# First chunk of a fused attention and MLP kernel: segments on 128 folded columns in PSUM banks of their own, four blocks by token half, grouped warm-up products, one listed order

## The chip, the cores and the metric

One NeuronCore of one Trainium2 chip runs the whole program. The metric is the device time of one execution in microseconds (us), as a median of several runs; smaller is better. The kernel before takes 912.23 us (three runs, 912.14 to 913.46).

## The reference

Sliding-window attention with a distance bias, then a two-layer MLP with squared relu, in float32 (the MLP's weights arrive as float64):

```python
B, H, S, D = 8, 8, 576, 64; window = 128
scores = q @ k.T / sqrt(D)
rel = pos[:, None] - pos[None, :]
scores = where((rel >= 0) & (rel < window), scores - slopes[h] * abs(rel), -1e9)
attn = softmax(scores)                       # per batch and head
x = (attn @ v).transpose(0, 2, 1, 3).reshape(B * S, H * D)   # 4608 x 512
out = (maximum(x @ w_in, 0) ** 2) @ w_out    # w_in 512 x 2048, w_out 2048 x 512
```

## The kernel before

The 4608 tokens form nine chunks of 512. Attention of a chunk is four head pairs; a pair has two segments of 256 queries. In the program's names, segment k = 0 to 7 belongs to the first chunk (pair k // 2, half k % 2 of the tokens), segments 8 to 15 to the second; q = 4 to 7 are the pairs of the second chunk and q = 8 is the first pair of the third. TensorE works in split precision: each product of float32 operands is three products of a high and a low part.

The MLP's first product of a chunk is sixteen blocks `g1` (one for each 128 columns of `w_in`; twelve products of 128 x 512), each followed by relu, square, a high part (`hh`) and a low part (`hl`). The second is sixteen blocks `g2`, twelve products each, summed in four PSUM banks. Sixteen weight units of 1 MB, `w` 0 to 15, arrive as float64 words on SyncE's queue and are turned into high and low parts in five steps `c` 0 to 4: a scaling on ScalarE (L204), a shift and a combine on VectorE (L206, L208), the high part on ScalarE (L210), the low part on VectorE (L212). A unit serves two blocks of `g1` or two of `g2`.

`start` records the first stage: attention of the first chunk, the MLP of the first chunk (`g1` 0 to 15, `g2` 0 to 13), the weights' conversion, attention of the second chunk and the scores of pair 8. `middle` records all that follows. Its first block of TensorE work is the last six products on the first chunk that the first stage leaves, then the second chunk's first `g1`; from there on the two kernels have the same work on TensorE. Every engine runs its instructions in the order in which they were recorded.

A first-chunk segment goes through `Wide`: scores `s` (L788) on up to 256 key columns per query block; four steps `u` (L798) that add a distance table to the scores in PSUM and take the row minimum; four exponentials `e` (L805) on ScalarE with their row sums; the reciprocals `r` (L436, L437); the scaling `n` (L818 on GpSimd, L816 on VectorE for one segment); transposes `z` (L825, L828) on TensorE; the copies `o` (L457, mostly ScalarE) and `m` (L832, VectorE) to SBUF; the product with the values `x` (L471); the high part `h` (L481, ScalarE) and the low part `l` (L484, VectorE). The segments run in the order 0, 1, 2 to 7. Pairs 4 to 8 use folded columns: the keys of a query's window lie in 128 columns by their position modulo 128; a copy `base` moves the scores to SBUF (L637, L644, ScalarE), and `fold` (L656, L660, VectorE) puts the older keys over the masked places. After the exponentials the folded tile goes through DRAM (`square`, `write`, `read`), and two selects (L508, GpSimd) part it into keys of the own and of the previous block, called `same` and `before`. `S` is a pair's scores (L584), `V` its product with the values (L520).

The order is set by a planner (`Plan.run`): each step has an engine, a duration, predecessors, a due time and the buffers it takes and frees, and a table of corrections `NUDGE`. One PSUM bank `g` serves `g1`; it is free when the relu has read it (L242). Warm-up products on zeros (`heat`, L160) fill TensorE in the first 32 us.

## Time and profile before

| what | value |
|---|---|
| time, median of 3 runs | 912.23 us (912.14 to 913.46) |
| profiled execution: span | 911.2 us, 1.0 us under that median |
| TensorE busy | 901.9 us of the span |
| VectorE, ScalarE, GpSimd busy | 579.5, 467.2, 259.6 us |
| granted TensorE clock | 1.00 throughout |

The page gives busy time for each engine, the span in 40 slices, and the chain that ended last. What matters here is where TensorE waits: it waits before 46 us and hardly after, so the stages have to be read apart. Other views give busy time in chosen stretches, single instructions in order of time, and the idle time ahead of groups of instructions with what ended it. An instruction's "us" includes a part that overlaps the next one's start; the distance between two starts is its pitch.

### The profile page before, as it was taken

Reading aid. Unit: us, or ns where it says so; the run is one execution under the profiler, and the core shown is the slowest. Engines: PE = TensorE matmul, PEld = TensorE weight load, DVE = VectorE, ACT = ScalarE, POOL = GpSimd, SP = SyncE. Lnnn points to the kernel's source line nnn. Section 1 sums busy time; section 2 is a strip of 40 time slices with the busy share of each in tenths; the row PEclk is TensorE's granted clock in tenths of the full one; section 3 lists DMA queues with packets and bytes.
Section 4 is the critical chain, followed back from the end, with each engine's and each line's share of the span. In section 5 each row is a group of like instructions: output and inputs, shape, how many; then the busy total and the mean of one; then the engine's idle time right before and its main releaser. Section 6 shows DMA issues by size and latency. Waiting matters only on the chain.

```text
span 911.2 us, 23218 instructions
## 1 busy us (share of the span) xinstructions
PE 901.9 (99%) x8500; PEld 799.2 (88%) x8500; DVE 579.5 (64%) x1596; ACT 467.2 (51%) x1321; POOL 259.6 (28%) x339
## 2 busy tenths in 40 slices
PE   9899999999999999999999999999999999999998
PEld 5688888888889999999999999999999999989997
DVE  6998882667776666565756665667666565654333
ACT  7898663566654445444544444445444454432222
POOL 4213235665522322213222322231322222230000
PEclk9999999999999999999999999999999999999999
DMA  9985226768888877877777778777887786667541
GB/s 347 404 312 171 88 62 210 243 211 275 296 278 293 292 253 260 262 246 221 233 279 247 216 236 267 250 227 243 271 258 229 244 261 195 193 207 224 171 126 47
DMA packets 137568, 212.95 MB, mean 234 GB/s; under 512 B 15216, under 2 KB 49392, under 8 KB 137456
## 3 DMA queue, kind: packets, MB, share of 16 engines
q1 hardware_dynamic: 137024, 210.96, 70.8%
q8 instruction: 68, 1.11, 0.5%
q10 hardware_dynamic: 432, 0.52, 0.2%
q14 instruction: 44, 0.36, 0.1%
HBM read 170.52 MB, written 40.89 MB: 232 GB/s over the span
## 4 chain that ended last, share of the span: by engine, by line
PE 95%; DVE 2%; DMA 1%; ACT 1%; issue 0%; POOL 0%; POOLq 0%; SPq 0%; DVEq 0%
PE acc L388 44%; PE chain L331 17%; PE rest L331 13%; PE g L233 9%; PE s L743 5%; PE g L756 2%; PE s L756 1%; PE at L520 1%; PE g L160 1%; DMA flow<-ws 1%; DMA pp<-way 0%; PE acc L471 0%; PE s L788 0%; PE acc L788 0%; DVE w L212 0%
## 5 line engine op out<-in xcount | busy, mean ns | idle before, releaser
L388 PE MATMUL acc<-hh,w 128*128 128x512 f32 x1152 | 405.3, 397 | 0.3 <-issue 0.3
L388 PEld LDWEIGHTS acc<-hh,w 128*128 128x128 f32 x1152 | 225.4, 196 | 39.5 <-issue 5.3
L388 PE MATMUL acc<-hl,w 128*128 128x512 f32 x576 | 227.4, 395 | 0.0
L336 DVE TENSOR_TENSOR four<-four,rest 128x256 f32<-128x256 f32 x112 | 47.2, 421 | 215.7 <-PE rest L331 214.6
L331 PEld LDWEIGHTS rest<-xu,flow 128*128 128x128 f32 x1008 | 143.8, 191 | 13.1
L508 POOL TENSOR_SCALAR_AFFINE_SELECT pp<-pp 128x512 f32<-128x512 f32 x128 | 95.5, 753 | 199.7 <-DMA pp<-way 163.3
L351 ACT COPY four<-chain 128x256 f32<-128x256 f32 x56 | 20.9, 373 | 251.4 <-PE chain L331 251.4
L331 PE MATMUL chain<-tees,flow 128*128 128x256 f32 x1008 | 147.5, 282 | 0.0
L331 PE MATMUL rest<-xu,flow 128*128 128x256 f32 x1008 | 146.7, 281 | 0.0
L441 POOL TENSOR_TENSOR t<-t,nm 128x512 f32<-128x512 f32 x64 | 69.6, 1090 | 256.8 <-DVE nm L437 162.5
L331 PEld LDWEIGHTS chain<-tees,flow 128*128 128x128 f32 x1008 | 132.2, 192 | 0.0
L388 PEld LDWEIGHTS acc<-hl,w 128*128 128x128 f32 x576 | 112.8, 196 | 12.8
L429 ACT ACTIVATE t<-t,nm 128x128 f32<-128x128 f32 x256 | 100.3, 395 | 8.9 <-DVE nm L422 8.3
L233 PE MATMUL g<-xu,w 128*128 128x512 f32 x384 | 95.2, 397 | 1.2 <-ACT r L242 1.2
L233 PEld LDWEIGHTS g<-xu,w 128*128 128x128 f32 x384 | 76.3, 209 | 14.3 <-ACT r L242 1.8
L422 DVE CUSTOM_DVE_ANT_0 t<-t,cst 128x128 f32<-128x128 f32 x256 | 63.1, 302 | 1.7
L251 DVE TENSOR_TENSOR hl<-r,hh 128x512 fp32r<-128x512 f32 x32 | 28.3, 883 | 43.1 <-ACT hh L249 43.0
L743 PE MATMUL s<-pp,v 64*64 64x128 f32 (+1 forms) x1792 | 52.3, 248 | 0.3 <-POOL pp L508 0.2
L331 PEld LDWEIGHTS chain<-xu,flow 128*128 128x128 f32 x336 | 48.7, 196 | 4.1
L656 DVE COPY_PREDICATED t<-cst,s 64x256 f32<-64x256 int32 x100 | 44.5, 445 | 11.8 <-PE s L743 5.4
L331 PE MATMUL chain<-xu,flow 128*128 128x256 f32 x336 | 49.4, 283 | 0.0
L429 ACT ACTIVATION_READ_ACCUMULATOR t<-t,nm 128x1 f32 x256 | 48.4, 189 | 0.0
(106 smaller groups left out, 1132.2 us busy)
## 6 DMA issues: line engine op xcount, KB each, us to landing
flow<-ws SPq DMA_DIRECT2D x392, 256.0 KB, 4.5
raw<-in_dram SPq DMA_DIRECT2D x32, 512.0 KB, 8.7
way<-pp SPq DMA_DIRECT2D x256, 64.0 KB, 2.2
pp<-way SPq DMA_DIRECT2D x64, 256.0 KB, 2.7
qk<-in_dram SPq DMA_DIRECT2D x32, 320.0 KB, 5.3
v<-in_dram SPq DMA_DIRECT2D x32, 320.0 KB, 4.6
qk<-in_dram SPq DMA_DIRECT2D x38, 256.0 KB, 5.1
out_dram<-o SPq DMA_DIRECT2D x35, 256.0 KB, 2.6
```

Source lines behind the costliest of these rows:

```text
L233: nc.tensor.matmul(g, w, xs[cc][:, part], start=i == 0, stop=i == 11)
L251: nc.vector.tensor_tensor(hl, r, hh.bitcast(F32), op=ALU.subtract)
L331: self.nc.tensor.matmul(to, w, x, start=start and k == 0, stop=k == 5, skip_group_check=True)
L336: add = lambda to, x: nc.vector.tensor_tensor(to, to, x, op=ALU.add)
L388: self.nc.tensor.matmul(self.acc[m], w, h, start=(f == 0 and i == 0), stop=(f == NF - 1 and i == 2))
L422: self.nc.vector.tensor_tensor_reduce(self.t[:, m], self.t[:, m], self.K.nrel(2 * self.p + m // 2), -0.125, BIG, ALU.add, ALU.min, self.nm ...
L429: return self.nc.scalar.activation(self.t[:, m], self.t[:, m], AF.Exp, bias=nm[:, 4 + m : 5 + m], scale=-1.0, accum_out=nm[:, m : m + 1],)
L441: self.nc.gpsimd.tensor_tensor(*(x.rearrange("p (j i) c -> p j i c", j=2) for x in (self.t, self.t)), self.rec.unsqueeze(3).to_broadcast([ ...
L508: nc.gpsimd.affine_select(to, self.own, pattern=[[-32 * sign, 4], [0, 4], [-sign, 32]], compare_op=op, fill=0.0, base=0, channel_multiplie ...
L656: nc.vector.copy_predicated(d, mask.unsqueeze(1).to_broadcast([64, 2, 2, 64]), e)
L743: yield self.nc.tensor.matmul(to, w, x, start=first and n < 2, stop=not first, skip_group_check=True)
L756: made = self.nc.tensor.matmul(to, w, x, start=not extra, stop=True, skip_group_check=True)
```

## The change

`Wide` becomes `Near`: the first chunk's segments use folded columns too. Scores are written by 64-row pieces, `fold` merges in PSUM, and `u` and `e` see 128 columns where they saw up to 256. The transposed tile is copied once (`o`), and two selects on GpSimd, `before` and `same`, make the two parts; the copy `m` is gone. Scores, transposes and value products have PSUM banks of their own (`low2`, `odd`, `sum1`) until the sums of `g2` take these banks over. The segments run as 0, 2, 4, 6 (first token half), then 1, 3, 5, 7. The tables `wide` (four loads of 256 KB) go; a select on GpSimd (`first`) makes a masked table from the shared one. For pairs 4 to 8 `base` goes too, and `merge` folds in PSUM.

```diff
+SEGMENTS = (0, 2, 4, 6, 1, 3, 5, 7)
+PSUBS = (0, 2, 12, 15)
+SUBS = (6, 7, 8, 9, 15, 16, 17, 21)
+HIGHS = (11, 15)
+HEATS = (7, 4, 4, 3, 8, 1, 3)
-HEAT = 16
-        (nc.gpsimd.tensor_copy if f in CASTS else nc.scalar.copy)(wh, flo)
-        nc.vector.tensor_tensor(wl, flo, wh.bitcast(F32), op=ALU.subtract)
+        (nc.gpsimd.tensor_copy if f in CASTS else nc.vector.tensor_copy if f in TRUNCS else nc.scalar.copy)(wh, flo)
+        (nc.gpsimd if f in PSUBS else nc.vector).tensor_tensor(wl, flo, wh.bitcast(F32), op=ALU.subtract)
...
+    def half1(self, u, s):
+        nc, cols = self.nc, slice(256 * s, 256 * s + 256)
+        g = self.g1.tile([128, 512], F32, name="g").rearrange("p (n t) -> p n t", n=2)
+        for n in range(2):
+            i = 0
+            for cc in range(NCC):
+                wl, wh = self.block(0, 2 * u + n, cc)
+                x = self.x[0, cc][:, :, cols]
+                for w, part in ((wh, 0), (wh, 1), (wl, 0)):
+                    nc.tensor.matmul(g[:, n], w, x[:, part], start=n == 0 and i == 0, stop=i == 11, skip_group_check=True)
...
+    def fold(self):
...
+        for h in range(2):
+            r = slice(64 * h, 64 * h + 64)
+            d = b[r, :, i, 64 * h : 64 * h + 64]
+            self.nc.vector.copy_predicated(d, self.K.mask[r].unsqueeze(1).unsqueeze(1).to_broadcast(list(d.shape)), e[r, :, i])
...
+    def unfold(self, own):
+        m = slice(1, 4, 2) if self.skip and not own else slice(0, 4)
+        to, sign = (self.own, -1) if own else (self.prev[:, m], 1)
+        self.nc.gpsimd.affine_select(
+            to, self.own[:, m], pattern=[[0, 2 if self.skip and not own else 4], [-sign, 128]], compare_op=ALU.is_ge if own else ALU.is_gt,
+            fill=0.0, base=0, channel_multiplier=sign,
+        )
...
+            P.add(n("before"), "Pool", 0.75 if sg else 0.4, (n("o"),), d - 1, do(G.unfold, False))
+            P.add(n("same"), "Pool", 0.75, (n("before"),), d - 1, do(G.unfold, True))
+            NF - 1: [("x", 6), ("x", 7)], ...
+            NF - 5: [("x", ends[1])], **{NF - 6 - u: [("g2", 2 * u + 1)] for u in range(HALVES)},
...
-            P.add(n("base"), "Activation", 0.6 if s else 1.3, (("S", q),) + first("base"), d + 5, do(C.begin, s), "t", "at" if s else None)
+            P.add(n("fold"), "DVE", 1.65 if late else 0.93, (("S", q),) + first("fold"), d, do(C.merge, s), "t")
...
-    return P.run()
+    return P.follow(ISSUE)
```

`half1` splits the first four blocks of `g1` by token half: `ga` 0 and 1 take two blocks each on tokens 0 to 255 (from segments 0, 2, 4, 6), `gb` 0 and 1 the same blocks on tokens 256 to 511; each is 24 products of 128 x 256. Their relu, square and parts are the steps `ha` and `hb`. In place of the planner's choice `start` follows a written list, `ISSUE`, so the order on every engine is fixed. The exponentials of pair 8 (eight `e`, sums and scaling) go from `start` to `middle`. The high part of two weight units moves to VectorE, three such steps come back from GpSimd to ScalarE, and the low parts of four units (`PSUBS`) and of several blocks (`SUBS`, `HIGHS`) go to GpSimd. Weight units 10 and 9 now lie where the parts of the first four blocks are kept, so their loads wait for `g2` 1 and 3. Thirty warm-up products in groups of 7, 4, 4, 3, 8, 1 and 3 stand where 32 stood in pairs.

On TensorE, where the first blocks begin, the kernel before has the scores of pair 4 (L584, cut here to their end), the last value product of the first chunk (L471, `pp`), `g1` 0 (`w_250`) and the first of pair 5's scores; `g1` 1 follows these:

```order
L584 MATMUL at<-qk 64x128
L584 MATMUL s<-qk 64x64
L471 MATMUL acc<-pp,v__242 64x128 x8
L233 MATMUL g<-xu,w_250 128x512 x12
L584 MATMUL at<-qk 64x128 x2
```

In the changed kernel the first half-token block `ga` 0 (L319, `w_224`) stands behind the value product of segment 1 (L567, `pw_98`), and the transposes of segments 5 and 7 (L932, `tw_95`, `tw_96`) and the value product of segment 3 (`pw_99`) stand behind it:

```order
L932 MATMUL odd<-cst,tw_94 128x128 x4
L567 MATMUL sum_117<-pw_98,v 64x128 x8
L319 MATMUL g<-xu,w_224 128x256 x24
L932 MATMUL at<-cst,tw_95 128x128 x4
L567 MATMUL sum_117<-pw_99,v 64x128 x8
L932 MATMUL odd<-cst,tw_96 128x128 x4
```

The first block has moved ahead of three value products and of pair 4's scores; the last of these products (segment 7) stands between `ga` 1 and `gb` 0, which is followed by pair 5's scores and `gb` 1.

On ScalarE the same stretch of the changed kernel, from the last exponential of segment 7 to its high part, reads as follows, in two pieces (L525 is `e`, L261 a weight's high part, L255 a weight's scaling, L553 is `o`, L577 is `h`, L299, L304 and L306 are relu, square and high part of `ha`; the names' numbers tell the units apart):

```order
L525 ACTIVATE tw_96,nm<-tw_96,nm 128x128
L261 CAST w_287<-raw_286 128x1024
L255 ACTIVATE raw_446<-raw_446 128x1024
L553 COPY pw_100<-at 128x512
L255 ACTIVATE raw_490<-raw_490 128x1024
L577 CAST xu<-sum_117 128x256
L553 COPY pw_101<-odd 128x512
L299 ACTIVATE r<-g 128x512
L304 ACTIVATE r<-r 128x512
L255 ACTIVATE raw_412<-raw_412 128x1024
L577 CAST xu<-sum_117 128x256
L306 CAST h_102<-r 128x2x256
```

and goes on with:

```order
L261 CAST w_342<-raw_341 128x1024
L255 ACTIVATE raw_370<-raw_370 128x1024
L299 ACTIVATE r<-g 128x512
L577 CAST xu<-sum_117 128x256
L304 ACTIVATE r<-r 128x512
```

The second fence goes on where the first ends; its L577 row is the high part of segment 7. In the kernel before, this high part stood behind the scalings of four units and one high part of a weight (L204 and L210) only:

```order
L204 ACTIVATE raw_355<-raw_355 128x1024
L481 CAST xu<-acc 128x256
L204 ACTIVATE raw_388<-raw_388 128x1024
L210 CAST w_292<-raw_291 128x1024
L481 CAST xu<-acc 128x256
L637 COPY t<-at 128x512
```

So seven scalings, three high parts of weights and four steps of `ha` now stand ahead of segment 7's high part, where four and one stood.

On SyncE's queue the first loads of the changed kernel are the first-half queries and keys, the table, the values, then weight unit 0 (`raw_223`), the second halves and unit 1 (`raw_286`):

```order
L167 DMA v__205<-in_dram 128x512
L249 DMA raw_223<-in_dram 128x1024 x2
L167 DMA qk<-in_dram 128x512 x3
L167 DMA qk__186<-in_dram 128x512
L249 DMA raw_286<-in_dram 128x1024 x2
```

Before, all loads of the first chunk and the four `wide` tables stood ahead of unit 0.

More of the change, by code (lines that the diff above doesn't have):

```diff
@@ L765, in two @@
             self.K.tc.add_manual_dep(made.ins, self.gate.ins.name, SYNC, reason="halves of the keys change banks")
-class Wide(Segment):
+class Near(Segment):
     def __init__(self, K, k):
         super().__init__(K, k)
-        self.skip = int(self.sg == 0)
-        self.first = [128 if self.skip and i == 0 else 0 for i in range(2)]
+        self.skip, self.turns = int(self.sg == 0), SEGMENTS.index(k)
     def scores(self):
@@ L824, in turn @@
         for m in range(4):
[L825 to L832 removed]
+            self.nc.tensor.transpose(self.z[:, m], self.t[:, m], self.K.ident)
@@ L857, in room, with follow @@
         self.count[name] = [0.0] * n
+    def follow(self, text):
+        names = [x[0] if len(x) == 1 else (x[0], *map(int, x[1:])) for x in (y.split(".") for y in text.split())]
+        assert sorted(names, key=str) == sorted(self.steps, key=str), set(names) ^ set(self.steps)
+        done = set()
+        for name in names:
+            engine, us, after, due, do, take, free, lag = self.steps[name]
+            assert done.issuperset(after), name
+            if do:
+                do()
+            done.add(name)
     def run(self):
@@ L874, in run @@
                     other = self.steps[a][0] != engine
-                    t = max(t, end[a] + HAND.get(self.steps[a][0], 0.15) * other + lag)
+                    t = max(t, end[a] + (HAND.get(self.steps[a][0], 0.15) if other else self.same * (engine in VECTOR)) + lag)
                 if any(not self.count[r] for r in take):
@@ L962, in start @@
-        P.add(n("h"), "Activation", 0.4, (n("x"),), d + 2, G.high)
-        P.add(n("l"), "DVE", 0.36, (n("h"),), d + 2, G.low, None, "xa")
+        after = [("q", c, p, 0), ("q", c, p, 1)][: sg + 1] + ([("s", SEGMENTS[i - 1])] if i else [])
+        chain = lambda s: ((s, SEGMENTS[i - 1]),) if i else ()
+        d, slot, turned = 4.0 * i, "sa" if i % 2 else "sc", "zp" if i % 2 else "at"
+        P.add(n("s"), "PE", 0.85 if sg else 0.92, tuple(after), d, G.scores, slot)
+        if not sg:
+            P.add(("first", p), "Pool", 0.5, ("nrel" if p else "near",), -1, do(K.table, p))
@@ new lines, in start @@
+        P.add(n("z"), "PE", 0.62, (n("n"),) + chain("z"), d - 3, G.turn, (turned, "pw"), "tw")
+        P.add(n("o"), *(("DVE", 0.6) if k in COPIES else ("Activation", 0.48)), (n("z"),), d - 2, G.out, None, turned)
+        P.add(n("before"), "Pool", 0.75 if sg else 0.4, (n("o"),), d - 1, do(G.unfold, False))
+        P.add(n("same"), "Pool", 0.75, (n("before"),), d - 1, do(G.unfold, True))
+        P.add(n("x"), "PE", 1.05 if sg else 0.82, (n("same"), ("v", c, p)) + chain("x"), d + 4, G.values, "xa", "pw")
@@ L964, in start @@
+        P.add(n("h"), "Activation", 0.27, (n("x"),), d + 2, G.high)
+        P.add(n("l"), "DVE", 0.34, (n("h"),), d + 2, G.low, None, "xa")
         if sg == 1:
@@ new lines, in start @@
+    for u in range(HALVES):
+        g = K.half1(u, 0)
+        P.add(("ga", u), "PE", 2.88, (*have(0), ("c", UNIT(0, 2 * u), n)) + ((("ga", u - 1),) if u else ()), GO, lambda g=g: next(g, None), "g")
+        after(("ha", u), 16 + u, g)
+    last, todo, f2 = {1: (), 2: ()}, [], 0
+    for u in range(HALVES):
+        todo.append(("gb", u))
+        if u:
+            todo += [("g2", f2), ("g2", f2 + 1)]
+            f2 += 2
+    for f in range(2 * HALVES, NF):
+        todo.append(("g1", f))
+        if f >= 2:
+            todo.append(("g2", f2))
+            f2 += 1
@@ L1280, in _consts @@
         cst[:, 256 + 128 * a : 384 + 128 * a] = -rel * (8 * slope(a))
-    later = r[:, None] < r[None, :]
-    near = [cst[:, 256 + 128 * a : 384 + 128 * a] for a in range(H)]
-    return np.concatenate([cst] + [np.where(late, t, np.float32(NEG)) for t in near for late in (later, ~later)], axis=1)
+    return cst
 def _arrays(q, k, v, moe_w_in, moe_w_out):
```

396 lines of the change are left out of this document (253 added, 143 removed), and 6 rows, old and new, of the table NUDGE.

## The prediction

> **What bounds the kernel now.** I looked first at busy time by stretch, because a mean over the span hides where TensorE waits. Columns are the stretch in us, its length, the busy time of PE, PEld, DVE, ACT and POOL, the granted clock, the DMA share and GB/s:
>
> ```profile
> 0.00:46.00 46.00, 41.14 (x392) 27.32 (x392) 36.67 (x136) 36.98 (x107) 14.93 (x19) 1.00 0.99 376
> 46.00:139.25 93.25, 93.17 (x627) 78.17 (x628) 80.07 (x171) 72.31 (x158) 29.73 (x35) 1.00 0.47 153
> 139.25:240.00 100.75, 100.75 (x878) 86.02 (x876) 59.64 (x147) 57.76 (x141) 59.79 (x70) 1.00 0.76 249
> ```
>
> From 46 us TensorE works without a pause: 93.17 of 93.25 us, then all of it. Time can only be won ahead of 46 us, and whatever is won there can be lost again by a wait behind it. The chain that ended last shows what follows that point (start, us, engine, line, count):
>
> ```profile
> 46.08 3.08 PE g L233 x12
> ...
> 106.60 2.80 PE acc L388 x12
> ...
> 110.87 3.15 PE g L233 x12
> ...
> 132.94 1.90 PE at L520 x32
> 134.84 4.41 PE acc L388 x18
> 139.25 2.79 PE g L233 x12
> ```
>
> At 46.08 the third `g1` begins. A block costs 2.80. A pair's scores cost 1.47 (from 106.60 + 2.80 to 110.87), a pair's value product 1.90. At 139.25 the second chunk begins; both kernels have the same TensorE work behind it. So I compare the moment at which **four `g1` blocks, all of the first chunk's attention and the scores of pairs 4 and 5** are done: before, these are done, by count of work, at 46.08 + 2 x 2.80 = 51.7 us. What is left from there is the same in both.
>
> TensorE's own order ahead of that point (the last value product, `g1` 0 and `g1` 1):
>
> ```profile
> 35.05 1.09 PE L471 MATMUL acc<-pp,v__242 128*64 128x128 f32 x16 [0.56 <-DVE xu L484]
> 36.08 3.21 PE L233 MATMUL g<-xu,w 128*128 128x512 f32 x12
> ...
> 42.25 3.09 PE L233 MATMUL g<-xu,w 128*128 128x512 f32 x12 [0.42 <-ACT r L242]
> ```
>
> The first block waits for the whole attention of the chunk. A value product takes 1.03.
>
> **The change: the new order to the same point.** ScalarE is the engine with the longest list up to there, so I add its pitches (start to next start) from its rows in order of time:
>
> ```profile
> 6.42 0.40 ACT L805 ACTIVATE tw<-tw,nm 128x128 f32<-128x128 f32 x1 [3.10 <-DVE nm L798]
> ...
> 13.15 0.59 ACT L457 COPY pp<-at 128x512 f32<-128x512 f32 x1 [0.17 <-PE at L825]
> 13.63 0.51 ACT L805 ACTIVATE tw<-tw,nm 128x256 f32<-128x256 f32 x1
> ...
> 16.71 0.37 ACT L481 CAST xu<-acc 128x256 fp32r<-128x256 f32 x1 [0.17 <-PE acc L471]
> 16.98 0.41 ACT L805 ACTIVATE tw<-tw,nm 128x128 f32<-128x128 f32 x1
> ...
> 22.82 1.15 ACT L204 ACTIVATE raw<-raw 128x1024 f32<-128x1024 f32 x1
> 23.86 0.57 ACT L457 COPY pp<-at 128x512 f32<-128x512 f32 x1
> ...
> 43.81 0.39 ACT L429 ACTIVATE t<-t,nm 128x128 f32<-128x128 f32 x1
> ...
> 44.20 0.39 ACT L429 ACTIVATE t<-t,nm 128x128 f32<-128x128 f32 x1
> ...
> 45.43 0.60 ACT L242 ACTIVATE r<-g 128x512 f32<-128x512 f32 x1
> 46.06 0.63 ACT L247 ACTIVATE r<-r 128x512 f32<-128x512 f32 x1
> 46.73 0.62 ACT L249 CAST hh<-r 128x512 fp32r<-128x512 f32 x1
> 47.25 1.16 ACT L210 CAST w<-raw 128x1024 fp32r<-128x1024 f32 x1
> ```
>
> `o` 0.48, `h` 0.27, a weight's scaling 1.04, an exponential on 128 columns 0.39, relu 0.63, square 0.67, high part 0.52; a weight's high part 1.16 less the same overlap of 0.11, 1.05. An exponential on 256 columns took 0.49 to 0.51 in its own row, so the 32 exponentials are also shorter than before.
>
> *The start.* Rows of TensorE and of VectorE's narrow fold:
>
> ```profile
> 1.30 3.88 PE L160 MATMUL g<-zero 128*128 128x512 bf16 x8 [1.30 <-DVE zero L155]
> 5.11 0.93 PE L788 MATMUL s<-qk 64*128 64x128 f32 x8
> ...
> 39.98 0.30 DVE L660 COPY_PREDICATED t<-cst,s 64x128 f32<-64x128 int32 x1
> ```
>
> Seven warm-up products instead of eight end at 1.30 + 7/8 x 3.88 = 4.7; scores 0.93; from their end to the first exponential it was 6.42 - 6.04 = 0.38; two folds add 0.65. First exponential: **6.7** (6.42 before).
>
> *To the first block `ga` 0.* It stands behind segment 1's value product, which needs segment 1's `o`. Ahead of and with that `o` ScalarE has 24 exponentials, five `o`, three `h`, two scalings and one high part: 9.4 + 2.4 + 0.8 + 2.1 + 1.05 = 15.7. To this come three waits. (a) Segment 2's reciprocals stand on VectorE ahead of segment 4's first `u`, and wait for segment 2's last exponential; so segment 4's first exponential is late by a reciprocal (0.35), a `u` (0.22) and handovers: 0.9. (b) Unit 0 has to land for its scaling. The loads:
>
> ```profile
> 0.00:10.00 10.00, 7.95 (x38) 3.16 (x38) 4.22 (x27) 5.07 (x17) 1.12 (x6) 1.00 0.83 282
> 10.00:20.00 10.00, 10.00 (x90) 6.85 (x90) 8.04 (x45) 9.32 (x36) 7.49 (x7) 1.00 1.05 398
> 20.00:30.00 10.00, 10.00 (x101) 7.19 (x100) 9.16 (x29) 9.25 (x29) 4.82 (x5) 1.00 1.03 404
> 30.00:40.00 10.00, 8.71 (x108) 6.59 (x106) 9.29 (x18) 7.68 (x13) 1.50 (x3) 1.00 1.03 405
> ...
> 40.26 1.32 ACT L204 ACTIVATE raw<-raw 128x1024 f32<-128x1024 f32 x1 [0.85 <-DMA raw<-in_dram]
> ```
>
> Up to unit 0 the new queue holds 3.80 MB (2.75 of queries, keys, values and tables, 1.05 of weights; 5.4 before). At 2.82 MB by 10 us and 398 GB/s these have moved by 12.5. Landing comes later: the unit that ScalarE waited for at 40.26 had 14.0 MB up to its end, and 14.9 had moved by 40, a lag of 2.1 us. Bounds 12.5 and 14.6; I take 13.4, nearer to the lower end, since the queue is short at that time. The scaling's turn comes at 12.2, so 1.2 (0.3 to 2.4); segments 2, 4 and 6's `o` and exponentials are queued behind it, and GpSimd's selects wait for these. (c) Unit 1 ends 2.1 MB later, at 18.6; its turn comes at 18.6 as well: 0 (to 1.2). With 0.3 for small handovers `o` ends at 6.7 + 15.7 + 0.9 + 1.2 + 0.3 = 24.8.
>
> GpSimd then does a select, a scaling (segment 3's) and a select before segment 1's value product:
>
> ```profile
> L818 POOL TENSOR_TENSOR tw<-tw,nm 128x512 f32<-128x512 f32 x4 | 4.2, 1043 | 0.0
> ...
> L441 POOL TENSOR_TENSOR t<-t,nm x64: 1042/1046/2022, 50.3 to 798.2; 128x512 f32<-128x512 f32 x64
> ...
> L508 POOL TENSOR_SCALAR_AFFINE_SELECT pp<-pp x128: 727/727/1581, 61.7 to 808.7; 128x512 f32<-128x512 f32 x128
> ```
>
> (the last two: minimum, median, maximum in ns). 0.73 + 1.04 + 0.73 and four handovers of 0.15: 3.1. Value product 1.03, so **`ga` 0 begins at 29.0**, 7 us ahead of `g1` 0 before.
>
> *From there TensorE's own work sets the time.* A half-token block has 24 products of 256 columns, priced by a group of six:
>
> ```profile
> 280.43 0.72 PE chain L331 x6
> ```
>
> 4 x 0.71 = 2.84. `ga` 0, two sets of transposes (0.5 each, an estimate: half of a value product's 16 records), three value products, pair 4's scores and `ga` 1: 2.84 + 1.0 + 3.1 + 1.47 + 2.84 = 11.2, so segment 7's value product ends at 40.2. Its `h`, `l` (0.34 by VectorE's pitch) and handovers, 1.1: 41.3. ScalarE's list up to that `h` is 32 exponentials, eight `o`, eight `h`, seven scalings, three high parts and four steps of `ha`: 12.5 + 3.8 + 2.2 + 7.3 + 3.15 + 2.45 = 31.4; with the waits above and 0.7 for segment 5's `o`, whose transposes now stand behind `ga` 0, it ends at 41.2, and `l` at 41.7. The two chains meet; I take 41.6 for `gb` 0. `gb` 0, pair 5's scores and `gb` 1 are 7.15, with 0.25 until a relu frees the one bank `g`: **49.0**, against 51.7.
>
> *Behind that point* TensorE has the same work, and 2.7 us less for everyone else. Two waits can take some of it. Units 9 and 10 now load only when `g2` 3 is done (49.0 + 5 x 2.80 = 63.0). Unit 9's scaling stands on ScalarE behind the square of `g1` 5, at about 67.5; behind it stand five other steps (2.7) and the relu that frees the bank for `g1` 7: 67.5 + 1.04 + 2.7 + 0.63 = 71.9, where `g1` 7's turn comes at 63.0 + 3 x 2.80 + 1.90 = 73.3, so there is 1.2 of room with a handover. Time to landing for these loads:
>
> ```profile
> DMA to landing us min/median/max: 3.8/8.7/11.8
> ```
>
> With little else on the queue then, I take 4.5 (bounds 3.8 and 8.7: nothing, or 3.0 on TensorE). And pair 7's value product stands 6 blocks, 1.90 and 1.47 behind its scores, 20.2, where it had 132.94 - 110.87 = 22.1; the chain between loses a copy to SBUF for each half (about an `o` each, 1.0 in all) and TensorE did not wait for it before, so I put it 0.3 late, with bounds of 0 and 0.9. I charge 0.6 for both: gain **2.1 us**.
>
> Costed at nothing: the warm-up products (TensorE waits there anyway; 0.49 each otherwise); `base` gone behind 46 us, where no wait of TensorE's hangs on it; VectorE's folds, covered by the removed copies `m` and by low parts that go to GpSimd; pair 8's exponentials in `middle` (ScalarE 57.8 of 100.75 us busy there; 3.1 without that cover).
>
> [...] GpSimd's operations above ran up to 2022 and 1581 ns, twice their minimum. [...]
>
> **The rivals.** Forecast, 912.23 - 2.1 = 910.1, chance 0.40 (909.0 to 911.2 by itself).
> *ScalarE hardly waits* (unit 0 lands by queue time, handovers hide): `ga` 0 some 2 us earlier and ScalarE 2.5 earlier, and nothing is given back: 907.3. For it: its rows before show waits of 0.17 only. Chance 0.23.
> *Weights land late*: units 0 and 1 at the upper ends cost 1.2 + 1.2 ahead of everything: 912.5. For it: the lag at 40.26. Against: the queue is shorter. Chance 0.15.
> *The gain is won and given back*: unit 9 or the way through DRAM makes TensorE wait 1.5: 911.6. Chance 0.10.
> *Slower: GpSimd becomes the bound*. Two selects a segment and the low parts go there; at the longest durations the three operations ahead of `ga` 0 cost 0.98 + 2 x 0.85 = 2.7 more and an earlier scaling 0.98, and `ga` 0 begins that much later: 913.8. It decides from 2.1 us in sum, about 0.5 for each of the four. Against: the scalings of the first 46 us took 1043. Chance 0.12.
>
> **How the numbers follow.** A measurement of this kernel can tell 0.2%, 1.8 us, from no change. Below 910.4 lie two thirds of the forecast's chance and the second case: 0.27 + 0.23 = 0.50. Within lie the rest of the forecast and two cases: 0.13 + 0.15 + 0.10 = 0.38. Slower by more: 0.12, though half of that case ends near its point of decision. The range 907.0 to 913.4 leaves out some 0.05 at the fast end and half of the slow case, and takes in the bounds of the landing.
>
> **What would show it.** First exponential near 6.7; unit 0's scaling waiting for its load about 1 us; `ga` 0 at 29, `gb` 0 at 41 to 42, `gb` 1's end at 49; TensorE without a pause from there to `middle`, whose first `g1` begins at about 137.1. It is wrong if `gb` 0 begins beyond 44 (GpSimd's or the weights' rows say which), or if TensorE pauses behind 49 for `r`, `raw` or `pp`.

## The result and the profile after

The changed kernel takes **918.37 us** (median of six runs, 915.38 to 920.52) against 912.92 for the kernel before beside it (six runs, 912.14 to 914.69): ratio 1.0057, 95% interval 1.0038 to 1.0076. It is slower by 0.57%, where 910.1 with a range up to 913.4 was predicted. The profiled execution took 917.32 us with a span of 915.6, so 4.4 us more than the profile before. Its six runs spread over 5 us, those of the kernel before beside them over 2.6.

First the same three stretches as before (stretch, length, busy time of PE, PEld, DVE, ACT, POOL, clock, DMA share, GB/s):

```profile
0.00:46.00 46.00, 40.66 (x463) 30.21 (x467) 34.35 (x150) 36.95 (x105) 25.00 (x33) 1.00 0.83 315
46.00:139.25 93.25, 91.58 (x677) 77.00 (x674) 70.19 (x167) 55.89 (x123) 35.66 (x32) 1.00 0.55 181
139.25:240.00 100.75, 98.27 (x858) 83.26 (x858) 61.28 (x141) 58.63 (x151) 62.80 (x73) 1.00 0.71 231
```

Behind 46 us TensorE no longer works through: it lacks 1.7 us of the second stretch and 2.5 of the third, where it lacked 0.1 and nothing. What it waited for, over the whole span (total, times, longest):

```profile
PE acc L466 <- ACT o L477: 2.5, 1, 2.5
PE g L284 <- ACT r L299: 1.7, 2, 1.3
PE s L897 <- DVE raw L257: 1.5, 1, 1.5
...
PE s L845 <- issue: 0.5, 1, 0.5
PE acc L466 <- issue: 0.5, 1, 0.5
```

L466 is a product of `g2`, L477 the copy of a finished PSUM bank to SBUF ahead of its store, L299 the relu. "Issue" means that the profile shows nothing that was waited for. The chain that ended last shows where this stands against the kernel before (start, us, engine, line, count):

```profile
29.52 3.79 PE g L319 x24
38.00 3.10 PE g L319 x24
42.13 3.79 PE g L319 x24
47.28 3.10 PE g L319 x24
50.38 2.80 PE acc L466 x12
...
139.71 2.79 PE g L284 x12
...
150.78 2.77 PE g L284 x12
153.58 0.61 ACT r L299
154.21 0.64 ACT r L304
154.87 0.62 ACT hh L306
155.48 0.49 ACT o L477
156.02 2.52 PE acc L466 x9
...
164.06 2.97 PE acc L466 x12
```

At the point that the prediction compares, the end of `gb` 1, the new kernel stands at 50.38 against 51.7: **1.3 us ahead**. At the second chunk's first `g1` it stands at 139.71 against 139.25: **0.5 behind**, so 1.8 went in between. The last row is the `g2` block behind the first visit of attention; in the kernel before it began at 160.64:

```profile
160.64 3.00 PE acc L388 x12
```

Now it is 3.4 behind. By 280 us it has won back 0.5 of that, and from there to 690 us the distance stays at 2.9; it grows by 0.6 and 0.9 at the two "issue" rows, which stand at 698 and 722 us, and is 4.3 at the end.

The loss at 153.58 reads thus: TensorE has finished a `g1` and its next product needs the PSUM bank of the first chunk's last output block. The copy that empties this bank stands on ScalarE behind relu, square and high part of that very `g1`. In the kernel before, the same copy (L399) stood one block earlier, at 150.64, ahead of the relu at 153.12:

```profile
150.64 0.59 ACT L399 COPY o<-acc 128x512 f32<-128x512 f32 x1 [1.13 <-DMA out_dram<-o]
153.12 0.60 ACT L242 ACTIVATE r<-g 128x512 f32<-128x512 f32 x1 [1.89 <-PE g L233]
```

The copy is the planner's work, in `middle`. The change gave `middle` pair 8's exponentials, sums and scalings, and so pair 8's write and read come later on SyncE's queue (143.80 instead of 139.77), with the stores of the output behind them (151.92 instead of 147.68). A copy needs one of four output buffers. By the planner's count two are held by early copies of weight blocks (GpSimd, to the same buffers) and two by the first two copies of the chunk, whose stores now come later; so none was free in time.

The loss at 102 us:

```profile
99.26 1.22 ACT L255 ACTIVATE raw<-raw 128x1024 f32<-128x1024 f32 x1 [2.37 <-DMA raw<-in_dram]
...
101.90 0.59 ACT L299 ACTIVATE r<-g 128x512 f32<-128x512 f32 x1
```

Weight unit 15's scaling waits 2.37 us for its load, and the relu that frees the bank `g` is queued behind it; TensorE loses 1.3. The load had been issued at 92.43, on SyncE's queue behind two writes and two reads of the way through DRAM. The remaining 0.4 of the L299 row is the same at 75 us, where unit 9's scaling waits 1.53 for its load.

### The profile page after: what moved, and what is told of

It reads as the page before. It is cut to its first block, busy times and chain, and to the rows that moved or that the text cites. A ratio compares the mean times of both kernels' runs of the same rounds, so it can differ in the third digit from the quotient of the medians.

```text
span 915.6 us, 23440 instructions
## 1 busy us (share of the span) xinstructions
PE 901.0 (98%) x8618; PEld 801.1 (87%) x8618; DVE 571.6 (62%) x1611; ACT 453.5 (50%) x1297; POOL 280.2 (31%) x355
## 3 DMA queue, kind: packets, MB, share of 16 engines
q8 instruction: 69, 1.13, 0.5%
## 4 chain that ended last, share of the span: by engine, by line
PE 92%; DMA 4%; ACT 1%; DVE 1%; SPq 1%; issue 1%; ACTq 0%; POOLq 0%; DVEq 0%
PE acc L466 43%; PE chain L406 18%; PE rest L406 13%; PE g L284 7%; PE s L845 5%; PE g L858 2%; DMA raw<-in_dram 2%; PE g L319 2%; PE s L858 1%; DMA way<-pp 1%; DMA qk<-in_dram 1%; DMA cst<-in_dram 1%; PE sum L567 1%; PE at L616 0%; PE at L680 0%
## 5 line engine op out<-in xcount | busy, mean ns | idle before, releaser
L466 PE MATMUL acc<-hh,w 128*128 128x512 f32 x1120 | 395.4, 398 | 3.0 <-ACT o L477 2.5
L466 PEld LDWEIGHTS acc<-hh,w 128*128 128x128 f32 x1120 | 219.3, 196 | 42.2 <-issue 6.1
L466 PE MATMUL acc<-hl,w 128*128 128x512 f32 x560 | 221.2, 395 | 0.0
L537 POOL TENSOR_TENSOR t<-t,nm 128x512 f32<-128x512 f32 x64 | 67.6, 1059 | 243.8 <-DVE nm L533 150.7
L466 PEld LDWEIGHTS acc<-hl,w 128*128 128x128 f32 x560 | 109.8, 196 | 12.0
L525 ACT ACTIVATE t<-t,nm 128x128 f32<-128x128 f32 x256 | 100.4, 395 | 9.6 <-DVE nm L500 9.0
L284 PE MATMUL g<-xu,w 128*128 128x512 f32 x336 | 83.0, 396 | 1.7 <-ACT r L299 1.7
L284 PEld LDWEIGHTS g<-xu,w 128*128 128x128 f32 x336 | 66.8, 209 | 13.0 <-ACT r L299 2.4
L500 DVE CUSTOM_DVE_ANT_0 t<-t,cst 128x128 f32<-128x128 f32 x216 | 52.8, 300 | 1.7
L845 PE MATMUL s<-pp,v 64*64 64x128 f32 (+1 forms) x1792 | 52.3, 248 | 0.7 <-issue 0.5
L589 DVE STREAM_TRANSPOSE pp<-t 128x512 f32<-128x512 f32 x64 | 45.2, 707 | 9.0 <-POOL t L537 5.8
L525 ACT ACTIVATION_READ_ACCUMULATOR t<-t,nm 128x1 f32 x256 | 48.6, 190 | 0.0
L299 ACT ACTIVATE r<-g 128x512 f32<-128x512 f32 x32 | 19.2, 599 | 53.3 <-PE g L284 44.9
```

The costliest lines, as they stand in the source:

```text
L284: nc.tensor.matmul(g, w, xs[cc][:, part], start=i == 0, stop=i == 11)
L466: self.nc.tensor.matmul(self.acc[m], w, h, start=(f == 0 and i == 0), stop=(f == NF - 1 and i == 2))
L500: self.nc.vector.tensor_tensor_reduce(self.t[:, m], self.b[m] if self.b else self.t[:, m], self.K.nrel(2 * self.p + m // 2), -0.125, BIG, ...
L525: return self.nc.scalar.activation(self.t[:, m], self.t[:, m], AF.Exp, bias=nm[:, 4 + m : 5 + m], scale=-1.0, accum_out=nm[:, m : m + 1],)
L537: self.nc.gpsimd.tensor_tensor(*(x.rearrange("p (j i) c -> p j i c", j=2) for x in (self.t, self.t)), self.rec.unsqueeze(3).to_broadcast([ ...
L589: nc.vector.transpose(squares.rearrange("p b m c -> p m b c"), self.t.rearrange("p m (b c) -> p m b c", c=32))
```

## Experiments: the two waits

Theory A: the late copy costs most of it. Theory B: unit 15's scaling costs 1 to 1.3. Rival C: the loss lies in the early part or in contention, and these waits are only where it shows. Beside all of the runs below but `copy_soon` the kernel before took 913.4.

**Pair 8 back in the first stage** (`e8_back`); `middle` is the kernel before's again:

```diff
-HAND = {"SP": 2.0, "PE": 0.3, "free": 0.0}
+HAND = {"SP": 2.0, "PE": 0.25, "free": 0.0}
...
-t.17.2 t.17.3 same.14 ... t.16.3 g1.15
+t.17.2 t.17.3 e.17.0 e.17.1 e.17.2 e.17.3 same.14 ... t.16.3 r.17 n.17 e.16.0 e.16.1 e.16.2 e.16.3 r.16 n.16 g1.15
...
-            first = min(ready, key=lambda r: (r[0], r[1], rank[r[2]]))
+            first = min(ready, key=lambda r: (r[0], r[1], str(r[2])))
...
-        chain(8, s, 0.0)
+        turned(8, s, 4.0 + 3 * s, ())
```

The edit also sets back a hand-over time of the planner (`HAND`) and its rule for ties. With these two alone set back, singly or together, the planner, which needs no chip, still puts the copy where the changed kernel has it; so it is pair 8's steps that move it.

> Pair 8's exponentials, sums and scalings stand in the first stage again, and the later stage plans as in the kernel before, so the copy-out of the first chunk's last bank stands on ScalarE right behind the other copy and not behind one more block's relu, square and high part. Theory A (this order costs the wait of 2.5 us and some 0.5 around it): the wait of TensorE for that copy is 0.2 or less, and the time is 918.4 - 3.0 = about 915.4. Theory B (unit 15's scaling ahead of a relu) alone: 918.4 unchanged. Rival C (the loss is in contention on GpSimd and VectorE or in the loads, wherever the copy stands): 918, the lost time shows in other waits.

Measured: 914.03 us, ratio 1.0011 (0.9996 to 1.0026), no wait for the copy.

**The same part alone, put into the kernel before** (`e8_alone`: the reverse edit, with the changed kernel's `middle`):

> The kernel before with one part of the change alone: pair 8's exponentials, sums and scalings in the later stage, planned as in the changed kernel. Theory A: TensorE waits about 2.5 us for the late copy here too, and the time is 912.9 + 3 = about 915.9. Theories B and C: 912.9, no change, since nothing else moves.

Measured: 917.44 us, ratio 1.0044 (1.0028 to 1.0061), with the wait:

```profile
PE acc L388 <- ACT o L399: 2.5, 1, 2.5
```

Done alone, this part makes the kernel before 4.0 us slower; undone, it makes the changed one 4.3 us faster. Handing pair 8's steps to `middle` is what costs, as theory A has it, and the early part isn't needed for it. Yet a wait of 2.5 us costs 4. Where the rest goes, three stretches of `e8_alone` show (the clock is the third number from the right):

```profile
151.97:155.38 3.41, 0.93 (x5) 0.47 (x4) 0.69 (x2) 2.33 (x4) 2.74 (x3) 1.00 0.98 368
155.38:158.80 3.42, 3.42 (x9) 2.68 (x10) 0.60 (x2) 0.00 (x0) 1.30 (x2) 0.50 0.77 291
158.80:162.21 3.41, 3.41 (x30) 2.62 (x32) 0.00 (x0) 0.24 (x1) 0.19 (x1) 1.00 0.47 174
```

TensorE was busy in 0.93 of 3.41 us; for the next 3.42 its granted clock is 0.50: another 1.7 us lost. The changes of the clock in a trace lie a whole number of stretches of 3.41 us apart (in `heat_less`, further on, it changes at 8.72, 15.54, 22.38 and 25.78 us). In the profiled execution of the changed kernel, counted back from the fall that its trace has just behind the end, at 916.45 us, the same wait lay across two such stretches, and the clock stayed at 1.00:

```profile
151.86:155.28 3.42, 1.68 (x8) 1.08 (x6) 0.00 (x0) 1.64 (x3) 1.63 (x3) 1.00 0.74 281
155.28:158.69 3.41, 2.67 (x11) 2.07 (x12) 1.29 (x2) 0.69 (x2) 1.75 (x2) 1.00 1.01 381
```

All six runs of `e8_alone` have a mean clock of 0.997 or 0.998 over the span; those of the changed kernel have 0.995 to 1.000, and the three lowest are the three slowest. So the profile that I read shows less loss than the median has. Ten falls within the program stand in the twenty traces, each behind a stretch of 3.41 us in which TensorE was busy for 0.93 to 1.68 us (0.93 above; 0.94 in `unit0_later` and 1.68 in `heat_less`, both further on). Of the 5266 stretches at full clock ahead of TensorE's last product that no fall followed, only the changed kernel's above (1.68) lay under 1.73. So it turns near 1.7 us of busy time: an estimate from the 1.68 and the 1.73.

**The copy alone** (`copy_soon`; the kernel before beside it 912.69): pair 8 stays in `middle`, and only the two early copies of weight blocks wait for the chunk's last copy, so a buffer is free for it.

```diff
-todo = ([("o", POOL, 0.65, early)] if apart else []) + ...
+todo = ([("o", POOL, 0.65, early + ((('give', 0, 3),) if j < 4 else ()))] if apart else []) + ...
```

> The changed kernel with pair 8's exponentials still in the later stage; only the two early copies of weight blocks on GpSimd wait for the first chunk's last copy-out, so an output buffer is there for it sooner and it stands on ScalarE one step of a block earlier (behind relu and square of the second block instead of behind the whole third block). Theory A (the place of the copy alone costs the time): TensorE's wait of 2.5 us falls to 1 or less, and with it the drops of the clock that follow; 918.4 - 3 = about 915. Rival (pair 8's eight exponentials load ScalarE there): the wait stays 2.5 and the time 918.

Measured: 915.86 us, ratio 1.0035 (1.0021 to 1.0050). The copy ran at 150.80, and TensorE's wait for it is gone altogether, not only shortened. So the wait came from the copy's place and not from the load of eight exponentials. The median falls by 2.5, though, and not by the 4.3 that `e8_back` gave. Where the other 1.8 goes isn't shown: the profiled execution, at 919.64, is the slowest of the twelve, with an "issue" pause of 2.1 at 723 us and a fall of the clock behind it.

**Unit 15's scaling later** (`e15_later`, and with `e8_back` as `both_back`):

```diff
-c.13.3 c.15.0 t.12.3
+c.13.3 t.12.3
-h1.10.3 c.13.4
+h1.10.3 c.15.0 c.13.4
```

> The changed kernel with weight unit 15's scaling on ScalarE behind the relu, square and high part of block 10 instead of ahead of them. Theory B: TensorE's wait of 1.27 us for that relu near 102 us goes, and the time falls by 1.0 to 1.3, to about 917.2. Theory A alone: the wait goes too, but what it gives is small beside the copy's. Rival C: the wait moves to another operation and the time stays 918.4.

> Both edits together. Theories A and B: 918.4 - 3.0 - 1.2 = about 914.2, by the profile a span within 0.5 us of the kernel before or below it. If the early reordering keeps its 1.3 us to the end: 911.6. Rival C: 917 or more.

Measured: 918.02 us (ratio 1.0049, 1.0031 to 1.0066) and 913.56 (1.0001, 0.9991 to 1.0011). In the first the relu came at 99.64 instead of 101.90 and the second chunk began at 138.88 instead of 139.71, so the wait's removal is worth 0.8; the copy's wait follows, five of six runs have a mean clock of 0.998 or less, and 0.35 is left in the median. Where the copy is mended, it is 0.5. Both are less than expected and lie within the intervals: that this wait went is shown, what it is worth in time is not. With both undone the kernel is level with the one before, not ahead. What else is there was the next question.

## Experiments: the early part

On top of `both_back`, each with the edits of the run ahead of it: unit 9's first two conversion steps behind block 6's relu and square (`nine_later`); unit 0's behind segment 6's steps `u` (`unit0_later`); three low parts of `ha` and `hb` back on VectorE (`parts_dve`).

```diff
-t.10.3 c.9.0 c.7.3 ... h1.6.1 g1.7
+t.10.3 c.7.3 ... h1.6.1 c.9.0 c.9.1 g1.7
...
-q.0.3.1 c.0.0 u.6.0 ... o.2 c.0.1 x.0
+q.0.3.1 u.6.0 ... o.2 x.0 e.4.2 u.6.3 before.2 e.6.0 c.0.0 s.3 heat.4 e.6.1 c.0.1
...
-SUBS = (6, 7, 8, 9, 15, 16, 17, 21)
+SUBS = (6, 7, 8, 9, 15)
```

> Both edits of the run that put pair 8 and unit 15 right, and unit 9's first two conversion steps moved behind the relu and square of block 6. The wait of 0.44 us for the relu near 75.7 goes: the time falls from 913.6 by 0.4 to 913.2. If the scaling's place doesn't matter there: unchanged, 913.6.

> As the run before, and unit 0's first conversion steps moved behind segment 6's steps u and the exponentials beside them, so that unit 0's landing at 14.3 us holds up neither ScalarE nor VectorE. If that landing sets the first block (the prediction's 1.2 us): TensorE's wait of 1.4 us near 13.6 goes, the first half-token block begins about 0.8 earlier than 30.0, time 912.4. Rival (GpSimd's selects or the order of segments sets it): the wait goes, the block stays at 29.5 to 30, time 913.2.

> As the run before, with the low parts of the three half-token steps (two of the first half, one of the second) on VectorE instead of GpSimd. Rival C (GpSimd's long operations there cost TensorE): 0.5 to 1 us less than the run before. Else: VectorE has 0.6 more for each of three and the last half-token block or its second product waits, 0 to 1 us more.

| run | us | ratio (95%) | read in the profile |
|---|---|---|---|
| `nine_later` | 913.24 | 1.0002 (0.9991 to 1.0012) | the wait near 75.7 gone; second chunk at 138.67, 0.6 ahead of the kernel before |
| `unit0_later` | 914.14 | 1.0011 (0.9998 to 1.0025) | wait at 14 us now for queries and keys; one of 2.5 at 24.7, put down to "issue" |
| `parts_dve` | 914.05 | 1.0015 (1.0005 to 1.0024) | median as `unit0_later` within 0.1 us; no wait at 24.7 |

Rival C's contention isn't borne out: with three of the long operations off GpSimd nothing is gained. Unit 0's landing was not what held the early scores back: when its steps stand elsewhere TensorE waits as long, 1.5 us, for queries and keys to land. The two best executions of `unit0_later` took 911.2 and 912.2, the slowest 918.1; the profiled one, 914.34, shows what can make the difference:

```profile
21.72:25.13 3.41, 0.94 (x12) 0.73 (x13) 1.29 (x7) 3.41 (x17) 1.71 (x3) 1.00 1.03 408
25.13:28.54 3.41, 3.41 (x39) 2.63 (x36) 2.38 (x12) 2.65 (x7) 2.62 (x5) 0.50 1.03 413
```

TensorE stood 2.46 us at a value product, and the clock was halved after it. The profile puts this wait down to "issue", but the other engines' rows show what ended it:

```profile
20.43 1.18 ACT L255 ACTIVATE raw<-raw 128x1024 f32<-128x1024 f32 x1 [2.20 <-DMA raw<-in_dram]
...
24.20 0.39 DVE L580 TENSOR_TENSOR xu<-sum,xu 128x256 fp32r<-128x256 f32 x1
...
24.70 1.18 PE L567 MATMUL sum<-pw,v 128*64 128x128 f32 x12 [2.46 <-issue]
```

Weight unit 1's scaling waits 2.20 for its load. Behind it stand the exponentials that VectorE's reciprocal waits for, and behind that the low part L580, which frees the bank `sum`; the product starts 0.11 after its end. In the changed kernel's own profile unit 1 had landed in time, and the same product starts 0.10 behind the same low part:

```profile
22.91 0.39 DVE L580 TENSOR_TENSOR xu<-sum,xu 128x256 fp32r<-128x256 f32 x1
...
23.40 0.88 PE L567 MATMUL sum<-pw,v 128*64 128x128 f32 x12 [0.46 <-DVE xu L580]
```

The long wait near 25 us is in six of the twenty profiles: `e8_back`, `unit0_later`, `halves_swapped` and three of the four shifts below. In these six unit 1's scaling waits 1.05 to 2.20 us for its load and the product starts 0.10 to 0.11 after the low part. In the other profiles of the new order it waits 0.69 at most. `e8_back` has the changed kernel's early order, so the load's landing differs between executions; why, no run shows.

**The price of a half-token block.** In all runs `ga` 0 and `gb` 0 took 3.79 and `ga` 1 and `gb` 1 3.10, where 2.84 was assumed. Of `ga` 0's 24 products (busy time of line L319 alone) 6 fall in the first 1.4 us and 13 in the next:

```profile
29.52:30.92 1.40, 1.40 (x6) 1.40 (x7) 1.00 1.00 398
30.92:32.32 1.40, 1.40 (x13) 1.40 (x14) 1.00 1.05 401
```

Block 0's first two weight pieces lie apart in memory, in every second column of the unit (`APART` in `block`), and take part in six products. With the two blocks of a step in the other order (`halves_swapped`):

```diff
-        for n in range(2):
+        for n in (1, 0):
...
-                    nc.tensor.matmul(g[:, n], w, x[:, part], start=n == 0 and i == 0, stop=i == 11, skip_group_check=True)
+                    nc.tensor.matmul(g[:, n], w, x[:, part], start=n == 1 and i == 0, stop=i == 11, skip_group_check=True)
```

> As the run with unit 0's steps later, with the two blocks of each half-token step in the other order. In all runs of the changed kernel the first six products of the first step and of the third were issued every 0.234 us and all others every 0.12. If this belongs to the two weight pieces of block 0 that lie apart in memory: the six slow products are now products 13 to 18 of those two steps, and a step still takes 3.8. If it belongs to the start of a step: the first six stay slow.

```profile
31.12:32.52 1.40, 1.40 (x12) 1.40 (x13) 1.00 1.04 400
32.52:33.92 1.40, 1.40 (x8) 1.40 (x7) 1.00 1.05 406
```

The slow products moved to the second half of the step, which still took 3.78. So it is these pieces: a product every 0.234 us where the others come every 0.12. A product of 512 columns takes 0.23 anyway (2.80 for the twelve of a block); in `g1` 0 of the kernel before, with the same six, only the first is late. At 256 columns it costs 0.7 in each of two steps.

## Experiments: TensorE's own instructions

Theory D: the "issue" pauses are loads of TensorE's instructions that come late. (The expectations of the next runs count the wait near 25 us among these.) The trace has the loads as transfers of 16 KB on a queue of their own, at 17.9, 27.9 and 38.1 us in the changed kernel and so on to the end (`q8 instruction: 69, 1.13` on its page, in packets and MB). Its TensorE has 17742 records of products and weight loads, 257 for each of the 69.

> As the run with unit 0's steps later, with 13 warm-up products instead of 30 (7 ahead of the first scores as before, then one in each of the six other places). What it asks: TensorE stood 1.9 and 2.5 us at the same value product near 22 us in two runs, waiting for no semaphore (the profile says issue), while its 16 KB loads of instructions arrive near 18.5 and 28.5 us. Theory D (the instructions arrive late for the dense part of the new order): 17 products less, so the point where the third load is needed lies some 34 instructions later in the program; the stall is shorter or gone, the runs spread less, and the median falls from 914.1 to about 912.5. Rival (the products keep the clock up): TensorE's longer pauses ahead of 30 us bring a granted clock of 0.5 there in most runs, and the time is 915 or more. If neither: 914, and the warm-up products cost nothing, as the prediction had it.

> The kernel before with 16 narrow warm-up products (64 columns) added to its twelfth pair, at a place where TensorE waits anyway: only the position of all later work in TensorE's instruction stream moves, by 32 instructions. Theory D in its wider form (where a load of instructions ends in the program decides whether TensorE stands later): the short pauses without a semaphore near 694 us move or grow, 0.3 to 2 us, time 913 to 914. Rival (those pauses belong to the new order alone): no change, 912.7, and the pause of about 0.3 stays where it was.

The edit of `heat_less`:

```diff
-HEATS = (7, 4, 4, 3, 8, 1, 3)
+HEATS = (7, 1, 1, 1, 1, 1, 1)
```

`heat_less` took 916.04 us (1.0026, 1.0014 to 1.0039). The long wait near 25 us isn't in its profile, where unit 1 had landed in time. But the rival wins: without the warm-up products TensorE is idle enough to lose its clock for three stretches of 3.4 us ahead of 26 us. Its later pauses stand at 285 and 311 us.

```profile
5.30:8.71 3.41, 1.68 (x29) 1.13 (x29) 2.47 (x15) 1.66 (x9) 1.18 (x3) 1.00 1.00 337
8.72:15.54 6.82, 6.47 (x50) 4.79 (x53) 4.57 (x31) 3.44 (x14) 3.34 (x5) 0.50 1.05 398
15.55:22.37 6.82, 3.75 (x72) 2.76 (x66) 5.17 (x18) 6.82 (x21) 4.33 (x5) 1.00 1.03 406
22.38:25.78 3.40, 3.40 (x40) 2.70 (x36) 3.27 (x19) 2.65 (x13) 1.98 (x3) 0.50 1.02 405
```

`before_code` adds 16 narrow products to the kernel before, at 25.5 us, and leaves its order alone. It took 914.87 us, ratio 1.0016 (1.0008 to 1.0025): the pause of 0.26 near 694 is gone, and one of 1.47 has come at 671:

```profile
671.61 0.45 PE L746 MATMUL s<-pp,v 64*64 64x128 f32 x8 [1.47 <-issue]
```

Not all of it is the place of the code. The expectation has TensorE waiting at that place, but the kernel before shows no wait there; the products take 0.5 us, and the second chunk begins at 139.58 instead of 139.25. By 240 us this profile is 0.5 behind, it stays so up to 665 us, and the two pauses bring it to 1.95. Then I tried to put the place back by four products (`code_align` on `nine_later`, `code_align_unit0` on `unit0_later`), and, as that failed, to move it by 16, 32, 48 and 64 products on `nine_later`:

```diff
+        self.hot = getattr(self, "hot", 0) + 1
+        for i in range({4: 32}.get(self.hot, 0)):
+            self.nc.tensor.matmul(g[:, 0:64], self.zb[:, 0:128], self.zb[:, 0:64], start=True, stop=True)
```

> The run with pair 8, unit 15 and unit 9 put right, and four narrow warm-up products (64 columns) more near 20 us. TensorE's instruction records ahead of the second chunk are 2084 in the kernel before, 2332 in that run, and 2340 here, which is 2084 + 256: loads of instructions come every 256 or so, so all later work now lies against them as in the kernel before. Theory D: the pause at L845 near 718 us (0.26 to 2.12 us in all runs of the changed kernel, none in the kernel before) is gone, the one near 694 stays at about 0.3, the median falls from 913.2 by 0.5 to 1, to about 912.4, level with the kernel before or 0.3 below it. Rival (the pause belongs to the new order of the later work, not to the position): L845 still waits 0.3 to 2 us near 718, time 913.2.

> The same four products in the run with unit 0's steps later. Theory D: the pause near 718 goes here too; the early one (1.7 to 2.5 us at the value product near 22 us, where the dense new order reaches the next load of instructions) stays in some runs, so the best executions fall to about 909 and the median is 912.5 to 913.5. Rival as in the run beside it: 914.

> The run with pair 8, unit 15 and unit 9 put right, and 16 narrow warm-up products more ahead of 9 us, where TensorE waits: all later work lies 32 instructions further on. Theory D (the place of the loads of instructions against the work): the pauses without a semaphore move to another of the later stage's visits or change there, and the time follows their sum. Rival E (the transfers that run near 718 us hold up whichever load of instructions falls there): a pause of 0.3 to 2 us stays near 718 in all four shifts.

> The same with 32 products more near 13 us, 64 instructions further on. Theory D: as above, another place or none. Rival E: 0.3 to 2 us near 718.

> The same with 48 products more, 96 instructions further on. Theory D: as above. Rival E: 0.3 to 2 us near 718.

> The same with 64 products more, 128 instructions further on, half a load of 256. Theory D: as above; over the four the sum of the pauses lies between 0 and 3 us, and the one with the smallest sum has a time of 912.5 or less. Rival E: 0.3 to 2 us near 718, and all four at 913 to 914.

(The diff is that of `shift_32`. The ratios are those on record and not quotients of the medians: beside the four shifts the kernel before itself ran from 912.27 to 919.51. The pauses at 24 and 25 us are the wait for unit 1.)

| run | us | ratio (95%) | "issue" pauses in its profile, us (at) |
|---|---|---|---|
| `nine_later` | 913.24 | 1.0002 (0.9991 to 1.0012) | 0.4 (694), 0.3 (718) |
| `code_align` | 914.67 | 1.0023 (1.0008 to 1.0038) | 0.3 (694), 1.8 (720) |
| `code_align_unit0` | 915.20 | 1.0031 (1.0019 to 1.0043) | 0.8 (693), 1.2 (718) |
| `shift_16` | 916.41 | 1.0028 (1.0008 to 1.0049) | 2.1 (24), 1.4 (674), 1.4 (700) |
| `shift_32` | 913.19 | 0.9987 (0.9969 to 1.0005) | none |
| `shift_48` | 915.51 | 1.0011 (0.9993 to 1.0030) | 2.0 (25), 0.2 (30), 0.2 (504), 0.6 (528) |
| `shift_64` | 917.85 | 1.0039 (1.0023 to 1.0055) | 1.7 (25), 0.9 (480), 1.2 (505) |

The step back of four products failed as expected by the rival: the pause moved by just four products inside its burst (13 narrow products left behind it, where 9 were). But larger shifts carry the pauses from 718 us to 700, 528 and 505, the longer ones always into a burst of narrow products (L845, L848 after the edit), and the profile of `shift_32` has none. Rival E (the traffic near 718 us) falls.

Two counts over the twenty traces say what the late pauses are. Behind 250 us there are 28 of them, of 0.18 to 2.12 us. Each ends 2.2 to 2.5 us after the start of a 16 KB load. And if TensorE's records (products and weight loads) are numbered from the start, each pause stands at a number that leaves 189 to 193 when it is divided by 256: `nine_later` 14014 and 14526, `shift_16` 13502 and 14014, `shift_64` 9406 and 9918, the kernel before 13761. So TensorE stands at the border of a load until the load is there, and theory D holds for them; the six waits near 25 us leave anything from 2 to 194, end 0.6 to 10.9 us after the start of a load and aren't of this kind. The border stays at its number, and what an edit moves is the work that meets it. Yet the place alone doesn't settle the price: `code_align` has the borders of the kernel before again, 256 records further on, with the same 0.26 near 694, but 1.79 at 720 where the kernel before has nothing. And each run has one profile only, so how often a pause comes isn't shown. Most loads bring no pause: the changed kernel's trace has 69 loads and two late pauses. All 28 stand in bursts of narrow products or just behind them.

**Last**, on `shift_32`, pair 7's second write ahead of its first read on SyncE's queue, which the profile showed as the last wait ahead of the second chunk (0.7 us for pair 7's selects):

```diff
-square.14 read.15 g1.14 low.6 c.15.2 write.14
+square.14 g1.14 low.6 c.15.2 write.14 read.15
```

> The run with 32 more products, and on SyncE's queue pair 7's second write ahead of its first read. In that run the second write was issued at 124.33, only when the first read's wait was over, though its square had ended at 121.6; TensorE waited 0.72 us for pair 7's selects at 133.3. The write goes out at 121.8, 2.5 us earlier; the wait goes, and the time falls by 0.7 to about 912.5, level with the kernel before or up to 0.3 below it. Rival (the early part's other waits take it, or the pauses for instructions come back in other executions): 913.2.

Measured: 913.73 us (911.93 to 917.35), ratio 1.0011 (0.9998 to 1.0024). The wait is gone, the second chunk begins at 138.50, the profiled span is 910.9, and an "issue" pause of 0.5 is back. The median does not follow. No version was shown to beat the kernel before: `nine_later` and `shift_32` are level with it, and both are faster than the changed kernel.

## Why the prediction was wrong

**The early part was nearly right up to `ga` 0, and right by luck at `gb` 0.** First exponential 6.90 (predicted 6.7), unit 0's scaling waiting 0.83 (1.2), `ga` 0 at 29.45 (29.0), `gb` 0 at 42.06 (41.6). But the prediction lets `gb` 0 wait for segment 7's high and low parts, 1.4 behind that segment's value product, and it doesn't: it begins right behind the product, before the low part has run.

```profile
41.03 1.09 PE L567 MATMUL sum<-pw,v__205 128*64 128x128 f32 x16
42.06 3.86 PE L319 MATMUL g<-xu,w 128*128 128x256 f32 x24
42.58 0.42 DVE L580 TENSOR_TENSOR xu<-sum,xu 128x256 fp32r<-128x256 f32 x1 [0.89 <-ACT xu L577]
```

Its first nine products read the other three pairs. TensorE's own work from `ga` 0 took 12.6 where 11.2 was summed, and the two errors nearly cancel. The GpSimd rival didn't come about, nor, as far as three low parts on the other engine can tell (914.05 in `parts_dve`, 914.14 in `unit0_later`), contention between GpSimd and VectorE.

**A term was mis-sized: "4 x 0.71 = 2.84" for a half-token block.** They took 3.79, 3.10, 3.79 and 3.10, 13.8 in all instead of 11.4. The group of six that priced them reads weights that lie together; block 0's first two pieces don't. The other two, at 0.12 a product, took 3.10 with a first product of 0.23. At the end of `gb` 1 the gain was 1.3, not 2.7.

**The step that failed: "Costed at nothing: ... pair 8's exponentials in `middle` (ScalarE 57.8 of 100.75 us busy there)".** ScalarE had the time, as said. What the prediction did not ask is what a planner does with a changed list of steps: SyncE's writes and reads moved, the stores behind them, the output buffers with these, and one copy changed places with a block's relu. That cost 4.0 us alone. The share of busy time says nothing of that; the order of `middle`, which could be read beforehand, had the copy behind three more ScalarE steps.

**The second step that failed: "I charge 0.6 for both".** Unit 9's scaling did hold up a relu (0.4), as described; unit 15, in the same position with its load behind the way through DRAM, was not looked at and took 1.3. With these two came the prediction's own sign of being wrong, a pause behind 49 for `r`.

**What no term had.** A pause of TensorE was paid again where it left a stretch of 3.41 us with TensorE busy for 0.93 to 1.68 us and the granted clock was 0.50 in the next (1.7 us more), and the new place of the code gave pauses of its own. Unit 1's late landing, which had a term (nothing, with 1.2 as its bound) and a rival, didn't come in the changed kernel's profile and did, with up to 2.2, in six others. The falls of the clock and this landing differ between executions of one kernel; that they make the spread of 5 us is likely and not shown.

In sum, the change was forecast 2.1 faster and came out 5.5 slower, 7.6 apart. The early part accounts for 1.4 of that, the two weight waits for 1.2 beyond their charge (by the profile; the medians show less), pair 8's steps for 4.0 to 4.3; the remainder, 0.7 to 1.0, fits the late pauses.

The forecast and its range rested on the sentence that behind 49 us the two kernels have the same work on TensorE. They have; but the other engines' order was not the same, and 0.6 was a guess in place of reading it.

## What to carry to other kernels

When a step is handed from a written list to a planner, compare the planned order on every engine before and after, above all copies that free PSUM banks and what their buffers wait for; "that engine is half idle" is no price. Where TensorE is busy throughout, weigh a pause by what it does to the clock too (1.7 us more in `e8_alone`), and read several executions when their times spread. Where a wait is put down to "issue", look which instruction of another engine ended just before it, and whether a load of instructions was under way. If a kernel at this limit changes by a few tenths of a per cent after an edit that should do nothing, see whether "issue" pauses stand in bursts of narrow products, and try a few harmless instructions more ahead of them.

## What the runs showed of the hardware

- The granted clock fell to 0.50 for 3.41 us (in one case, in `heat_less`, 6.82) behind ten stretches of 3.41 us with TensorE busy for 0.93 (`e8_alone`) to 1.68 (`heat_less`) of them; of the other stretches ahead of TensorE's last product, one with 1.68 (the changed kernel) and all from 1.73 up brought no fall.
- TensorE paused 0.18 (`shift_48`) to 2.12 us (`copy_soon`) for its instructions, in bursts of narrow products or just behind them: 28 pauses, all at the same place modulo 256 records (189 to 193), all ending 2.2 to 2.5 us after the start of a 16 KB load. 32 instructions more ahead of them (`before_code`) moved the kernel before's pause from 694 to 671 us and made it 1.47 instead of 0.26.
- An accumulating product started 0.10 (the changed kernel) to 0.11 us (`unit0_later`) after the VectorE instruction that freed its bank, also where the profile said "issue".
- A product of 128 x 256 came every 0.12 us with weights that lie together and every 0.234 with weights in every second column (`ga` 0 of the changed kernel; `halves_swapped` has the same in the other order).
